# Loads of r and k without their pad rows, one more load in flight, and a re-drawn instruction order, in an RWKV-like attention fused with a gated MLP

## The chip, the cores and the metric

The kernel runs on one core of a Trainium2 chip. The metric is the time of one execution in microseconds (us) on the device; before the change three executions took 326.5, 326.91 and 327.86 us, median 326.91 us. All data are float32.

## What is computed

For 4 batches of 768 tokens, 8 heads of 48 dimensions run a linear recurrence over the tokens; its output, with the heads side by side, goes through a feed-forward layer that mixes along the tokens:

```python
for t in range(S):
    cur = np.einsum('bhd,bhe->bhde', u[None] * kt, vt)
    y[:, :, t] = np.einsum('bhd,bhde->bhe', rt, state + cur)
    state = w[None, :, :, None] * state + np.einsum('bhd,bhe->bhde', kt, vt)
...
h = np.maximum(x @ w_in, 0.0)                     # 384 -> 1024
u, v = h[..., :512], h[..., 512:]
v_n = (v - mean(v)) / sqrt(var(v) + 1e-06)
v_s = np.einsum('ts,bsd->btd', w_spatial, v_n) + b_spatial[None, :, None]
return (u * v_s) @ w_out                          # 512 -> 384
```

## The kernel before

**The work.** The recurrence is done in 24 chunks `m` of 128 tokens, six to a batch. Chunk `m` needs four loads: `rk` (r and k, dimension-major: 128 partitions of 4 KB, 512 KB), `rs` and `ks` (r and k, token-major, 192 KB each) and `rkv` (v, 384 or 512 KB). In `rk` each half of 64 partitions holds one head of each pair: 48 rows of data and 16 rows of zeros, which `dmajor` in `kernel` pads. `prep` (L587) then scales `rk` by powers of w, the k part on POOL (L595) and the r part on DVE (L597) in the first 13 chunks, in one DVE instruction (L601) later; forms `rs*ks*ub` (POOL L353 twice), reduces it per head on DVE (L607), scales `ks` (POOL L353) and spreads the sums on the tile `a` (L353). PE computes `scores` (L638, 32 small matmuls of rk with rk), `products` (L657, of ks with rkv) and `apply` (L719, 64 to 96 matmuls into the tile xp), and `fin` writes the result as a high and a low part, the tile x.

**The layer.** Every large product is done as three matmuls of high and low parts (`mm3`, L762 to L764): `moe_v` (L772, nine of 128x512), `moe_u` (L880, nine of 128x384; the first of all by parts at L892), the token mixing `moe_sp` (with combinations of quadrants, whose weights `wa`, `wb` are split in two parts by ACT and POOL, and whose inputs `t` are split by ACT and POOL or DVE at L358 and L353) and `moe_out`. The weights arrive as 64-bit words; `from_f64` (L475) turns w_in's six pieces of 512 KB into two parts on DVE, ACT and, for three of them, PE (L495 to L497).

**What sets the order.** Nothing runs in the order of the text. Every instruction is a task in `Plan` with the engines it may run on and a cost; `Plan.run` lists the tasks by due times, with models of the transfers (`landing`, with `SLOW`, `PART`, `TO_BYTE`), of PE's clock and its instruction loading, and writes each engine's program in that order. `shake` first moves the due times of random groups of tasks: one group for each number in `SEEDS`, so the numbers in that table set the order. All loads are issued by SP in the planned order (`load`, L367). `LANES` is the number of loads in flight: `run` adds a wait to every load for the one `LANES` loads before it (L300), and `lane` (L213) gives the planner the same rule. A load also waits until its buffer is free; `rk` has two buffers (`SLOTS`), rotated by `tile_of`.

**Names.** In the rows, `rk`, `rs`, `ks`, `rkv`, `wa`, `wb`, `t`, `X`, `a`, `A`, `x`, `xp`, `ps`, `pm` are tiles; `wa<-w_in` and `wb<-w_sp` are loads of weights. PE's L762 with x and wi is `moe_v` or `moe_u`, with wa or wb and t it is `moe_sp`.

Of the kernel before, what the change touches and what calls it, by code (L numbers as in the profile page):

```python
# [8 lines left out]
F32 = mybir.dt.float32  # L9
# [3 lines left out]
ALU = mybir.AluOpType  # L13
AX = mybir.AxisListType

B, H, S, D = 4, 8, 768, 48
# [3 lines left out]
P = 128  # L20
C = 128
# [3 lines left out]
NP = H // 2  # L25
# [14 lines left out]
LEAN = 4.0  # L40
AHEAD = 0.3
ALONE = 1000.0
CALM, LATE = 80.0, dict(DVE=1.0, SP=1.0)
SEEDS = (786675, 590737, 650567, 473966, 410529, 555426, 907183, 123843, 647820, 960324, 828658, 912501, 134089,
         159232, 4393, 523669, 612611, 964576, 241432, 346394, 906374, 371707, 92393, 507276, 798277, 338735, 176835,
         444512, 896537, 239246, 993420, 861971, 866320, 990367, 131959, 191835, 802215, 648123, 562279, 390339,
         978361, 670519, 812235, 451845, 697243, 382570,)
BIAS = dict(DVE=3.0, ACT=3.5)
MOST_IN, MOST_OUT = 2, 1

# [3 lines left out]
CHAIN = dict(PE=0.0, DVE=0.115, ACT=0.11, POOL=0.0, SP=0.0)  # L54
SWITCH = {"bs": 0.095, "br": 0.095, "by": 0.095, "sb": 0.215, "sy": 0.11, "rb": 0.105, "yb": 0.105}
STAY = 1.0
LANES = 6
PORT = dict(DVE=(0.07, 0.0, 0.0), POOL=(0.15, 0.06, 0.02))


# [58 lines left out]
class Plan:  # L119
# [1 line left out]

    SLOW, PART = 210e3, (6.0, 42.0)
    RATE, TO_BYTE, BEHIND_BYTE = (395e3, 395e3, 262e3), (2.2, 2.9, 1.3), (0.5, 0.5, 0.4)

    def __init__(self, slots, wait):
        self.wait, self.sent = wait, []
# [45 lines left out]
    def shake(self):  # L174
        for seed in SEEDS:
            rnd = random.Random(seed)
# [27 lines left out]
    def landing(self, line, at, nbytes):  # L204
        part = sum(at > x for x in self.PART)
        line = max(line, at + self.TO_BYTE[part])
        slow = min(nbytes / self.SLOW, max(0.0, 5.2 - line))
        line += slow + (nbytes - slow * self.SLOW) / self.RATE[part]
        return line, line + self.BEHIND_BYTE[part]

# [2 lines left out]
    def lane(self, at, landed):  # L213
        return max(at, landed[-LANES]) if len(landed) >= LANES else at

    def run(self):
# [8 lines left out]
        while ready:  # L225
# [71 lines left out]
            if way.nbytes:  # L297
                self.sent.append(made.ins)
                if len(self.sent) > LANES:
                    self.wait(made.ins, self.sent[-1 - LANES].name)  # L300
        assert all(t.end is not None for t in self.tasks)
# [3 lines left out]
def fused_kernel(ctx, tc, rkT, rkvE, rkvL, wT, uB, w_in, w_sp, b_sp, w_out, out):  # L305
# [9 lines left out]
    SLOTS = dict(rk=2, rs=2, ks=2, rkv=3, a=1, A=2, t=4, X=2, gt=4, u=8, vs=2, g=3, ob=2, pm=5, ps=1, xp=1, x=2, s=2, t1=1, dg=2, q=2)  # L315
    SLOTS |= {f"w{x}{n}": 1 for x in "ab" for n in range(NS)}
    const = ctx.enter_context(tc.tile_pool(name="const", bufs=1))
# [7 lines left out]
    plan = Plan(SLOTS, wait)  # L325
    T = {}

    def tile_of(key, shape, dtype=F32):
        key = key[:2]
        if key not in T:  # L330
            home = psum if key[0] in ("pm", "ps", "xp") else sbuf
            T[key] = home.tile(shape, dtype, name=key[0], tag=f"{key[0]}{plan.slot[key]}")
        return T[key]
# [6 lines left out]
    def dve(n, f, r, w, cost=None, two=False, due=None):  # L340
        plan.add([("DVE", n / 960 + 0.07 if cost is None else cost, f, two)], r, w).most = due
# [25 lines left out]
    def load(key, shape, dtype, src, nbytes, view=None, due=None):  # L367
        def f():
            t = tile_of(key, shape, dtype)
            return nc.sync.dma_start(out=view(t) if view else t, in_=src)  # L370
        plan.add([("SP", 0.45, f, False, nbytes)], (), [key], lag=0).most = due


    wt = const.tile([P, NP], F32, name="wt")
    ub = const.tile([P, DM], F32, name="ub")
    tt = const.tile([P, NP, C], F32, name="tt")
# [14 lines left out]
    def eye():  # L391
        return tile_of(EYE, [P, P])

    def neg(n=1):
        return tile_of(NEG, [P, 2, P], F32R)[:, n]
# [65 lines left out]
    TTP = ("pm", "tt")  # L461
    TN = [("c", "tn", 0), ("c", "tn", 1)]

    def load_chunk(m):
        b, c = divmod(m, NC)
        load(("rk", m), [P, 2, NP, C], F32, rkT[b, c], P * 2 * NP * C * 4)
        n, src = (ROW_E, rkvE[m]) if m < EC else (ROW, rkvL[m - EC])
        load(("rs", m), [P, DM], F32, src[:, 0:DM], P * DM * 4)
        load(("ks", m), [P, DM], F32, src[:, OK:OV], P * DM * 4)
        load(("rkv", m), [P, ROW - OV], F32, src[:, OV:n], P * (n - OV) * 4, lambda t: t[:, 0:n - OV])  # L470
# [116 lines left out]
    def prep(m):  # L587
        RK, RS, KS, DG, A = ("rk", m), ("rs", m), ("ks", m), ("dg", m), ("a", m)
        a = lambda: tile_of(A, [P, 2, 2, 2, HC])
        r_, k_, kn, rn = (RK + ("r",), RK + ("k",), KS + ("kn",), RS + ("rn",))  # L590
        rk = lambda: T[RK]
        TT = [("c", "t0"), ("c", "t1"), ("c", "t2")]
        if m < EARLY:
            for i, key in ((1, k_), (0, r_)):
                plan.add([("POOL", 1.24, lambda i=i: nc.gpsimd.tensor_tensor(  # L595
                    out=rk()[:, i], in0=rk()[:, i], in1=tt, op=ALU.mult), True),
                    ("DVE", 0.6, lambda i=i: nc.vector.tensor_tensor(  # L597
                        out=rk()[:, i], in0=rk()[:, i], in1=T[TTP].rearrange("p (n c) -> p n c", n=NP),
                        op=ALU.mult), False, 0, LEAN if i else -9.0)], [RK, TTP, *TT], [key])
        else:  # L600
            dve(1024, lambda: nc.vector.tensor_tensor(out=rk(), in0=rk(), in1=tt.unsqueeze(1).to_broadcast(  # L601
                [P, 2, NP, C]), op=ALU.mult), [RK, *TT], [r_, k_], cost=1.14, two=True)
        n_, k0 = (lambda: T[RS]), (lambda: T[KS])
        lean = ALONE if m < QUIET else LEAN
        pair(DM, lambda: dict(out=n_(), in0=n_(), in1=k0(), op=ALU.mult), [RS, KS], [rn], lean=lean)
        pair(DM, lambda: dict(out=n_(), in0=n_(), in1=ub, op=ALU.mult), [rn, ("c", "ub")], [rn], lean=lean)
        dve(DM - 8, lambda: nc.vector.tensor_reduce(out=tile_of(DG, [P, H]), in_=n_().rearrange("s (h d) -> s h d", h=H),  # L607
                                                axis=AX.X, op=ALU.add), [rn], [DG])
        pair(DM, lambda: dict(out=k0(), in0=k0(), in1=tn_f, op=ALU.mult), [KS, rn, *TN], [kn], lean=lean)
        pair(432, lambda: dict(  # L610
            out=a().rearrange("s b q z t -> s (b q z) t"), in0=diag.unsqueeze(1).to_broadcast([P, H, HC]),
            in1=T[DG].unsqueeze(2).to_broadcast([P, H, HC]), op=ALU.mult), [DG, ("c", "diag")], [A], lean=lean)
        if m >= EC:
            move(RK + ("r",), ("A", m), "r", [(64 * (1 - t), t, slice(2 * b, 2 * b + 2), 64 * (t ^ b))
                                              for b in range(2) for t in range(2)],
                 lambda p, h: rk()[h:h + 64, 0, p])
# [422 lines left out]
    for i in range(NM):  # L1039
        n = FIRST[i] if i < NC else len(steps) if i == NM - 1 else int(10 + (i - 5) * per / 6)  # L1040
# [20 lines left out]
    for b in range(B):  # L1061
        for c in range(NC):
            m = b * NC + c
# [93 lines left out]
```

## Time and profile before

| | before |
|---|---|
| three executions | 326.5, 326.91, 327.86 us |
| the profiled execution | 327.6 us, span 325.9 us |
| mean granted clock of PE | 0.995 |
| PE busy | 309.7 us, 95% |
| DMA, mean over the span | 151 GB/s, 49.14 MB |
| 24 loads of rk | 512 KB each, median 5.6 us from issue to landing |

The span runs from the first to the last instruction. PE is busy nearly all the time, so what counts is where it isn't, and what releases it there. A row of the waits or of a timeline tells how long an engine stood idle and which instruction ended that; "issue" is idle time that the profile gives no instruction for. The granted clock is a share of 2.4 GHz.

### The profile page before, as it was taken

The page shows a single profiled execution, that of the slowest core. Times are in us where ns is not written, and L with a number is a line of the kernel's source. Part 1 is how long each engine was busy: PE and PEld are TensorE (multiplying, and loading weights), DVE is VectorE, ACT ScalarE, POOL GpSimd, SP SyncE. Part 2 cuts the span into 40 slices and gives each one's busy share as a digit, 9 for nine tenths or more (in the row PEclk, how much of TensorE's full clock was granted, in tenths as well). Part 3 has the DMA queues.
Part 4 walks back from the last instruction along what each step waited for, and adds up shares of the span by engine and source line. Part 5 has one row for each costly group of instructions (what it writes and reads, how often), then busy time and mean ns, then how long its engine had stood idle before and what let it go on. Part 6 is the DMA issues. An engine that isn't in the chain of part 4 may idle for free.

```text
span 325.9 us, 10933 instructions
## 1 busy us (share of the span) xinstructions
PE 309.7 (95%) x4574; PEld 283.3 (87%) x4574; DVE 245.4 (75%) x465; ACT 198.6 (61%) x492; POOL 250.9 (77%) x235
## 2 busy tenths in 40 slices
PE   2787999999999999999999999999999999999995
PEld 1466788999999888998979998999988989999995
DVE  6899986799962899858999996489998431727830
ACT  4346984847643887767759477686576663433422
POOL 3878999999988999899999875688999440358700
PEclk9997999999999999999999999999999999999999
DMA  6999768685255836154346245264140010010013
GB/s 229 377 393 382 257 219 278 217 295 181 91 172 185 270 100 235 32 178 141 106 166 203 51 177 171 81 205 139 51 147 5 25 50 2 0 51 24 0 42 105
DMA packets 21233, 49.14 MB, mean 151 GB/s; under 512 B 2496, under 2 KB 12096, under 8 KB 21184
## 3 DMA queue, kind: packets, MB, share of 16 engines
q1 hardware_dynamic: 21040, 48.34, 43.2%
q8 instruction: 36, 0.59, 0.8%
q14 instruction: 13, 0.11, 0.1%
q10 hardware_dynamic: 144, 0.10, 0.1%
HBM read 43.58 MB, written 4.72 MB: 148 GB/s over the span
## 4 chain that ended last, share of the span: by engine, by line
PE 68%; DVE 10%; POOL 8%; DMA 7%; ACT 3%; issue 2%; SPq 0%; POOLq 0%; ACTq 0%; DVEq 0%
PE pm L762 20%; PE pm L764 19%; PE pm L763 19%; PE xp L719 5%; DMA rs<-rkvE 4%; PE ps L638 3%; POOL rs L353 2%; DMA rk<-rkT 2%; DMA wb<-w_sp 2%; PE ps L657 1%; DVE rk L601 1%; POOL wb L353 1%; DVE A L625 1%; POOL t L353 1%; DVE a L353 1%
## 5 line engine op out<-in xcount | busy, mean ns | idle before, releaser
L762 PE MATMUL pm<-wa,t 128*128 128x384 f32 x120 | 41.3, 344 | 0.0
L763 PE MATMUL pm<-wa,t 128*128 128x384 f32 x120 | 40.5, 337 | 0.0
L764 PE MATMUL pm<-wa,t 128*128 128x384 f32 x120 | 40.4, 336 | 0.0
L353 POOL TENSOR_TENSOR t<-vs,t 128x384 fp32r<-128x384 f32 x26 | 32.6, 1269 | 1.4 <-ACT t L358 1.4
L762 PE MATMUL pm<-x,wi_h 128*128 128x384 f32 x93 | 32.0, 344 | 0.0
L764 PE MATMUL pm<-x,wi_l 128*128 128x384 f32 x93 | 31.2, 336 | 0.0
L763 PE MATMUL pm<-x,wi_h 128*128 128x384 f32 x93 | 31.2, 336 | 0.0
L624 ACT COPY A<-rk 64x256 f32<-64x256 f32 x54 | 21.8, 404 | 15.1 <-PE xp L719 5.3
L353 POOL TENSOR_TENSOR rs<-rs,ks 128x384 f32<-128x384 f32 x21 | 26.8, 1276 | 4.4 <-DMA ks<-rkvL 2.9
L762 PE MATMUL pm<-wi_h,x 128*128 128x512 f32 x69 | 28.5, 413 | 0.3 <-DVE g L933 0.3
L762 PE MATMUL pm<-wo_h,gt 128*128 128x384 f32 x84 | 28.6, 340 | 0.0
L764 PE MATMUL pm<-wo_h,gt 128*128 128x384 f32 x84 | 28.3, 336 | 0.0
L763 PE MATMUL pm<-wo_l,gt 128*128 128x384 f32 x84 | 28.3, 336 | 0.0
L764 PE MATMUL pm<-wi_h,x 128*128 128x512 f32 x69 | 27.7, 401 | 0.0
L763 PE MATMUL pm<-wi_l,x 128*128 128x512 f32 x69 | 27.5, 399 | 0.0
L353 POOL TENSOR_TENSOR ks<-ks,tn 128x384 f32<-128x384 f32 x23 | 25.1, 1092 | 0.0
L353 POOL TENSOR_TENSOR rs<-rs,ub 128x384 f32<-128x384 f32 x22 | 23.4, 1062 | 1.3
L353 POOL TENSOR_TENSOR X<-vs,X 128x384 f32<-128x384 f32 x9 | 10.6, 1175 | 17.6 <-ACT vs L844 17.2
L933 DVE TENSOR_TENSOR g<-pm,bb 128x384 f32<-128x384 f32 x32 | 17.5, 549 | 8.6 <-PE pm L764 8.2
L353 POOL TENSOR_TENSOR a<-diag,dg 128x512 f32<-128x512 f32 x16 | 17.2, 1077 | 8.5 <-ACT A L624 7.6
L353 POOL TENSOR_TENSOR gt<-u,gt 128x384 fp32r<-128x384 f32 x20 | 22.6, 1142 | 1.3 <-ACT gt L358 1.3
L762 PEld LDWEIGHTS pm<-wa,t 128*128 128x128 f32 x120 | 22.6, 188 | 1.1 <-DVE g L933 0.6
(182 smaller groups left out, 960.4 us busy)
## 6 DMA issues: line engine op xcount, KB each, us to landing
rk<-rkT SPq DMA_DIRECT2D x24, 512.0 KB, 5.6
rkv<-rkvL SPq DMA_DIRECT2D x16, 512.0 KB, 3.8
out<-ob SPq DMA_DIRECT2D x23, 192.0 KB, 2.0
wa<-w_in SPq DMA_DIRECT2D x6, 512.0 KB, 5.5
rkv<-rkvE SPq DMA_DIRECT2D x8, 384.0 KB, 5.9
rs<-rkvL SPq DMA_DIRECT2D x16, 192.0 KB, 2.7
ks<-rkvL SPq DMA_DIRECT2D x16, 192.0 KB, 5.2
wb<-w_sp SPq DMA_DIRECT2D x6, 384.0 KB, 5.4
```

Of the source, the lines that this page charges most:

```text
L353: plan.add([(e, cost[e], lambda e=e: engine[e].tensor_tensor(**f()), True, 0, lean if e == "DVE" else 0.0) for e in ways.split()], r, w)
L601: dve(1024, lambda: nc.vector.tensor_tensor(out=rk(), in0=rk(), in1=tt.unsqueeze(1).to_broadcast([P, 2, NP, C]), op=ALU.mult), [RK, *TT], ...
L624: ("ACT", (n + 250) / 1200, lambda out=out, p=p, h=h: nc.scalar.copy(out(), source(p, h))),
L625: ("DVE", n / 1920 + 0.15, lambda out=out, p=p, h=h: nc.vector.tensor_copy(out=out(), in_=source(p, h)), True, 0, LEAN)],
L638: nc.tensor.matmul(ps[64 * hf:64 * hf + 64, b, o:o + HC], rk[hd, 1, p, s0:s0 + 64], rk[hd, 0, p, t0:t0 + 64], start=True, stop=True, skip_ ...
L657: nc.tensor.matmul(ps[64 * j:64 * j + D, b, o:o + D], kn[hs, kc:kc + D], ve[hs, h, z, p, slice(0, D) if m < EC else slice(16 * h, 16 * h + ...
L719: nc.tensor.matmul(xp[32 * p:32 * p + 32, o:o + HC], lhsT, rhs, start=p not in began, stop=True, skip_group_check=True, tile_position=(0, ...
L762: nc.tensor.matmul(o, lh, rh, start=first, stop=False, skip_group_check=free)
L763: nc.tensor.matmul(o, lh, rl, start=False, stop=False, skip_group_check=free)
L764: nc.tensor.matmul(o, ll, rh, start=False, stop=last, skip_group_check=free)
L933: dve(TH, lambda: nc.vector.tensor_tensor(out=g(K), in0=T[PM][:, 0:TH], in1=other(), op=ALU.add), [PM, ("c", "bb"), *r], [K])
```

## The change

The first load into each of the two `rk` buffers (chunks 0 and 1) brings all 128 rows. From chunk 2 on, `load_chunk` makes two loads, of rows 0 to 47 and 64 to 111, 192 KB each; the pad rows in the buffer stay as they are. For this the two buffers become fixed tiles (`pairs`) and the instructions that read `rk` depend on both loads. `LANES` goes from 6 to 7. In the planner's model of the transfers two constants and the bound 5.2 change, all for the first 6 us, and `SEEDS` is another list of 61 numbers instead of 46, so that every engine's order is another.

```diff
-LANES = 6
+LANES = 7
...
-    SLOW, PART = 210e3, (6.0, 42.0)
-    RATE, TO_BYTE, BEHIND_BYTE = (395e3, 395e3, 262e3), (2.2, 2.9, 1.3), (0.5, 0.5, 0.4)
+    SLOW, PART = 240e3, (6.0, 42.0)
+    RATE, TO_BYTE, BEHIND_BYTE = (395e3, 395e3, 262e3), (0.95, 2.9, 1.3), (0.5, 0.5, 0.4)
...
-        slow = min(nbytes / self.SLOW, max(0.0, 5.2 - line))
+        slow = min(nbytes / self.SLOW, max(0.0, 6.0 - line))
...
     def tile_of(key, shape, dtype=F32):
         key = key[:2]
+        if key[0] == "rk":
+            return T.setdefault(key, pairs[plan.slot[key]])
...
+    pairs = [const.tile([P, 2, NP, C], F32, name=f"rk{n}") for n in range(SLOTS["rk"])]
...
     def load_chunk(m):
         b, c = divmod(m, NC)
-        load(("rk", m), [P, 2, NP, C], F32, rkT[b, c], P * 2 * NP * C * 4)
+        if m < SLOTS["rk"]:
+            load(("rk", m), [P, 2, NP, C], F32, rkT[b, c], P * 2 * NP * C * 4)
+        else:
+            for h in range(2):
+                rows = lambda t, h=h: t[64 * h:64 * h + D]
+                load(("rk", m, h), [P, 2, NP, C], F32, rows(rkT[b, c]), D * 2 * NP * C * 4, rows)
...
-                        op=ALU.mult), False, 0, LEAN if i else -9.0)], [RK, TTP, *TT], [key])
+                        op=ALU.mult), False, 0, LEAN if i else -9.0)], [RK, RK + (0,), RK + (1,), TTP, *TT], [key])
...
-                [P, 2, NP, C]), op=ALU.mult), [RK, *TT], [r_, k_], cost=1.14, two=True)
+                [P, 2, NP, C]), op=ALU.mult), [RK, RK + (0,), RK + (1,), *TT], [r_, k_], cost=1.14, two=True)
```

`SEEDS` starts with 786675, 590737, 650567 before and with 510017, 789016, 349449 after.

What this does to the order, at three places. First SP's loads around those of chunks 2 and 3. Before, from the end of chunk 2's loads to chunk 3's `rk` (`rk_445`; the number behind a name tells the buffers' uses apart):

```order
L370 DMA rk_292<-rkT 128x1024
L370 DMA rkv_301<-rkvE 128x768
L370 DMA rs_311<-rkvE 128x384
L370 DMA wb2_348<-w_sp 128x768
L370 DMA ks_354<-rkvE 128x384
L370 DMA wb1_369<-w_sp 128x768
L370 DMA wb5_429<-w_sp 128x768
L370 DMA rs_434<-rkvE 128x384
L370 DMA wb0_437<-w_sp 128x768
L370 DMA rk_445<-rkT 128x1024
```

The same stretch of SP in the change, from chunk 2's `ks` on:

```order
L373 DMA ks_242<-rkvE 128x384
L373 DMA wb4_291<-w_sp 128x768
L373 DMA rk0_74<-rkT 48x1024 x2
L373 DMA rs_330<-rkvE 128x384
L373 DMA rkv_348<-rkvE 128x768
L373 DMA ks_359<-rkvE 128x384
L373 DMA wb0_365<-w_sp 128x768
L373 DMA wb2_424<-w_sp 128x768
L373 DMA wb5_428<-w_sp 128x768
L373 DMA wb3_434<-w_sp 128x768
L373 DMA wb1_438<-w_sp 128x768
L373 DMA rk1_75<-rkT 48x1024 x2
```

All six pieces of w_spatial now stand ahead of chunk 3's `rk`, four did before. Up to and with chunk 3's `rk` SP asked for 10114 KB before and asks for 10434 KB now; with chunk 2's `rk` it was 7106 and is 7362 KB, with chunk 2's `ks` 6082 and 6594 KB, with chunk 0's `rk` 1538 KB (the fourth load) and 2306 KB (the eighth).

Second PE at chunk 3. Before, from chunk 2's `apply` (the second row of L719 is its a part) to chunk 3's; the nine rows of `moe_v` of chunk 2 (`pm_635`) are cut to their first and last:

```order
L719 MATMUL xp_527<-a_442,rkv_193 32x64 x24
L657 MATMUL ps_81<-rkv_301,ks_354 48x48 x16
L638 MATMUL ps_81<-rk_445 64x64 x16
L762 MATMUL pm_635<-wi_h_82,x_294 128x512
L764 MATMUL pm_635<-wi_h_82,x_294 128x512
L719 MATMUL xp_657<-rk_445,A_114 32x64 x24
L719 MATMUL xp_657<-a_612,rkv_301 32x64 x24
L892 MATMUL pm_718<-x_294,wi_h_82 128x384 x6
```

The same place in the change, where the nine rows are those of `pm_612`:

```order
L728 MATMUL xp_519<-a_466,rkv_175 32x64 x24
L666 MATMUL ps_83<-rkv_348,ks_359 48x48 x16
L771 MATMUL pm_612<-wi_h_84,x_295 128x512
L773 MATMUL pm_612<-wi_h_84,x_295 128x512
L647 MATMUL ps_83<-rk1_75 64x64 x16
L901 MATMUL pm_654<-x_295,wi_h_84 128x384 x4
L728 MATMUL xp_664<-rk1_75,A_120 32x64 x24
L728 MATMUL xp_664<-a_601,rkv_348 32x64 x24
```

Chunk 3's `scores`, which need its `rk`, now stand behind chunk 2's `moe_v` instead of ahead of it, and four of the first `moe_u`'s matmuls stand ahead of chunk 3's `apply`. At chunk 2, `products` now stand ahead of `scores`, the other way round before.

Third POOL at the start of batch 1's token mixing, where the inputs t are made from v (`vs`). Before:

```order
L353 TENSOR_TENSOR vs_1707<-vs_2081,vs_1707 128x3x128
L353 TENSOR_TENSOR t_2432<-X_2416,t_2432 128x384
L353 TENSOR_TENSOR t_2436<-vs_2081,t_2436 128x384
L353 TENSOR_TENSOR wb5_2224<-X_2414,wb4_2186 128x384
L353 TENSOR_TENSOR X_2536<-vs_2081,X_2416 128x384
L353 TENSOR_TENSOR X_2554<-vs_1707 128x384
L353 TENSOR_TENSOR t_2556<-X_2536,t_2556 128x384
```

In the change:

```order
L356 TENSOR_TENSOR wb5_2370<-X_2402,wb4_2344 128x384
L356 TENSOR_TENSOR X_2467<-vs_1767 128x384
L356 TENSOR_TENSOR X_2491<-vs_2084,X_2467 128x384
L356 TENSOR_TENSOR t_2511<-X_2467,t_2511 128x384
L356 TENSOR_TENSOR t_2514<-vs_2084,t_2514 128x384
L356 TENSOR_TENSOR vs_1767<-vs_2084,vs_1767 128x3x128
L356 TENSOR_TENSOR X_2491<-vs_2084,X_2491 128x384
```

The last split of a weight (`wb5`) stands ahead of all of these instead of among them, the input of the fourth product (`X_2536` before, `X_2491` now) is made three instructions earlier, and its split is no longer on POOL.

## Rows read from the trace of the kernel before

**Rows 1.** page part 1: engine, busy us (share of the span), instructions
```profile
PE 309.7 (95%) x4574; PEld 283.3 (87%) x4574; DVE 245.4 (75%) x465; ACT 198.6 (61%) x492; POOL 250.9 (77%) x235
```

**Rows 2.** stretches of the span, their columns named in the first row
```profile
core 0: us, PE busy (x) PEld busy (x) DVE busy (x) ACT busy (x) POOL busy (x), PEclk, DMA share, GB/s
0.00:35.03 35.03, 23.64 (x583) 16.88 (x583) 30.49 (x59) 18.42 (x45) 25.67 (x37) 0.95 0.94 347
35.03:326.00 290.97, 286.08 (x3993) 266.41 (x3992) 214.94 (x407) 180.16 (x448) 225.18 (x199) 1.00 0.38 127
```

**Rows 3.** waits of PE after 35 us: engine line <- releaser: us, times, longest
```profile
PE pm L764 <- POOL t L353: 0.8, 1, 0.8
PE pm L762 <- DVE g L933: 0.3, 1, 0.3
```

**Rows 4.** stretches of 4 us and the last 6 us (columns as in group 2)
```profile
24.00:28.00 4.00, 1.94 (x67) 1.72 (x68) 4.00 (x9) 2.00 (x7) 3.66 (x5) 0.86 1.02 381
28.00:32.00 4.00, 4.00 (x61) 3.00 (x60) 3.96 (x9) 3.38 (x10) 3.59 (x4) 0.71 1.02 383
320.00:326.00 6.00, 2.27 (x13) 1.95 (x12) 0.36 (x1) 0.80 (x2) 0.00 (x0) 1.00 0.26 89
```

**Rows 5.** timeline of PE: start us, us, instruction xcount [idle before <-releaser]
```profile
25.34 0.30 PE L719 MATMUL xp<-a,rkv 128*32 128x64 f32 x2 [1.59 <-issue]
...
26.36 0.73 PE L638 MATMUL ps<-rk 64*64 64x64 f32 x32 [0.72 <-issue]
...
27.66 0.79 PE L762 MATMUL pm<-wi_h,x 128*128 128x512 f32 x1
...
33.01 0.58 PE L657 MATMUL ps<-rkv,ks 64*48 64x48 f32 x32
...
34.34 0.69 PE L638 MATMUL ps<-rk 64*64 64x64 f32 x32 [0.76 <-POOL rk L595]
...
34.97 0.50 PE L762 MATMUL pm<-wi_h,x 128*128 128x512 f32 x1
...
38.73 1.32 PE L892 MATMUL pm<-x,wi_h 128*128 128x384 f32 x6
```

**Rows 6.** chain that ended last, first 40 us: start us, us, piece
```profile
2.18 6.12 DMA rk<-rkT
```

**Rows 7.** tile rk on SP, 17.5 to 17.9 us: issue, then its time to landing
```profile
L370 SPq DMA_DIRECT2D rk<-rkT x1: 328/328/328, 17.6 to 17.6; - x1
...
DMA to landing us min/median/max: 6.0/6.0/6.0
```

**Rows 8.** tile rk on SP, 25.99 to 26.31 us, the same
```profile
L370 SPq DMA_DIRECT2D rk<-rkT x1: 328/328/328, 26.0 to 26.0; - x1
...
DMA to landing us min/median/max: 6.9/6.9/6.9
```

**Rows 9.** timeline of POOL, the start
```profile
21.16 1.02 POOL L353 TENSOR_TENSOR rs<-rs,ks 128x384 f32<-128x384 f32 x1 [1.27 <-DMA ks<-rkvE]
...
24.19 1.27 POOL L595 TENSOR_TENSOR rk<-rk,tt 128x512 f32<-128x512 f32 x1
...
25.72 1.04 POOL L353 TENSOR_TENSOR a<-diag,dg 128x512 f32<-128x512 f32 x1 [0.26 <-PE xp L719]
...
31.18 1.01 POOL L353 TENSOR_TENSOR wa<-wb,wa 128x384 fp32r<-128x384 f32 x1 [0.41 <-ACT wa L358]
...
33.01 1.27 POOL L595 TENSOR_TENSOR rk<-rk,tt 128x512 f32<-128x512 f32 x1 [0.82 <-DMA rk<-rkT]
```

**Rows 10.** timeline of POOL, 144 to 149 us
```profile
144.38 1.01 POOL L353 TENSOR_TENSOR wb<-X,wb 128x384 fp32r<-128x384 f32 x1
...
147.62 1.35 POOL L353 TENSOR_TENSOR t<-X,t 128x384 fp32r<-128x384 f32 x1
```

**Rows 11.** tile A on SP: its two 64-row DMAs of 64 KB, time to landing
```profile
L623 SPq DMA_DIRECT2D A<-rk x2: 462/498/534, 66.6 to 67.4; - x2
...
DMA to landing us min/median/max: 3.7/3.9/4.2
```

More of the change, by code (lines that the diff above doesn't have):

```diff
@@ L43 @@
 CALM, LATE = 80.0, dict(DVE=1.0, SP=1.0)
[L44 to L47, printed above, removed]
+SEEDS = (510017, 789016, 349449, 4415, 22282, 162314, 413315, 599960, 460165, 632294, 15888, 576524, 887186, 388971,
[4 rows of a table added]
 BIAS = dict(DVE=3.0, ACT=3.5)
```

4 rows, old and new, of the table SEEDS are left out of this document.

## The prediction

> **What bounds the kernel now.** I read the page's busy times first: PE works 309.7 us of a span of 325.9 us [rows 1], so 16.2 us are all that an order of instructions can still win. The stretches tell where they lie [rows 2]: in the first 35.03 us PE is idle for 11.4 us, in the other 290.97 us for 4.9 us. The waits of PE in that long part [rows 3] name only 0.8 us behind a POOL instruction and 0.3 us behind a DVE instruction; 3.7 us of the rest are the copy and the store after the last matmul, in the last 6 us [rows 4], which the change leaves as they are. So the long part is bound by PE's own work, which the change does not touch: the same matmuls, in another order. A time can come out differently by the first 35 us, by those 1.1 us, or by new waits.
>
> In the first 35 us the DMA engines are the bound: their share is 1.02 from 24 to 32 us [rows 4] and 0.94 over all of the stretch [rows 2], and what PE and POOL wait for are loads. POOL stood 1.27 us until chunk 2's `ks` had landed, and 0.82 us until chunk 3's `rk` had [rows 9]; PE waited 0.76 us for that `rk` to be scaled by POOL [rows 5]. Ahead of that it had stood 1.59 and 0.72 us with no instruction named ("issue") [rows 5], and then the granted clock fell: 0.86 and 0.71 of full speed from 24 to 32 us [rows 4], 1.00 in all that comes later [rows 2]. That is 4 x 0.14 + 4 x 0.29 = 1.7 us of PE's work lost at the lower level, 1.2 GHz.
>
> **The change part by part.** *When the loads land.* I take the landings as a function of the kilobytes that SP has asked for. Chunk 0's `rk` completes 1538 KB and lands at 2.18 + 6.12 = 8.3 us [rows 6]; chunk 2's 7106 KB at 17.6 + 6.0 = 23.6 us [rows 7]; chunk 3's 10114 KB at 26.0 + 6.9 = 32.9 us [rows 8]. That is 5568 KB in 15.3 us, 364 KB/us, and then 3008 KB in 9.3 us, 323 KB/us. With the new list: chunk 2's `ks` (6594 KB) lands at 8.3 + 5056/364 = 22.2 us, its `rk` (7362 KB) at 23.6 + 256/323 = 24.4 us, chunk 3's `rk` (10434 KB) at 23.6 + 3328/323 = 33.9 us; at 364 KB/us it would be 32.7 us. So at the place that matters the smaller loads bring nothing earlier: 2 x 128 KB are saved up to there, but two more pieces of w_spatial, 768 KB, have been put ahead.
>
> *Chunk 0's `rk`* lands 768 KB later, 2.1 us. I cost it at nothing: 4288 KB, 11.8 us of transfers, lie between it and the next load that anything waited for, chunk 2's `ks`. Without that cover it costs up to 2.1 us.
>
> *Chunk 2.* POOL starts on it at 22.2 instead of 21.16 us; three instructions later, 24.19 - 21.16 = 3.03 us, it scales `rk`, at 25.2, which takes 1.27 us [rows 9]. `scores` can start at 26.5 us; they started at 26.36 us [rows 5], 0.9 us after POOL was done. I call that level; the hold before them stays, since it stands at the same place of PE's program, and with it the lower clock.
>
> *Chunk 3, the term of the sum.* `products` of chunk 2 now run ahead of `scores`, while POOL still scales `rk`, so `moe_v` of chunk 1 starts at about 26.5 + 0.6 = 27.1 instead of 27.66 us. From there to the end of chunk 3's `products` it took 33.01 + 0.58 - 27.66 = 5.9 us [rows 5], so they end at 33.0 us. Before, PE now had `scores` of chunk 3 in front of it and waited. In the change it has chunk 2's `moe_v`. That and chunk 3's `apply` took 38.73 - 34.97 = 3.8 us, the `scores` 0.6 us, four of the six matmuls at L892 about 0.8 us [rows 5]; x of chunk 2 comes about 0.3 us late. The sum is 33.0 + 5.5 = 38.5 us, with the four matmuls done. Before, `apply` ended at 38.73 us and the four came behind it: 39.5 us. The gain is 1.0 us, and 1.3 us if x is in time; I take **1.2 us**. `scores` don't wait: POOL has as many instructions ahead of chunk 3's scaling as before (8.0 us from 24.19 to 32.19 us [rows 9], so free by 33.2 us), starts it when `rk` lands, 33.9 us, and ends it at 35.2 us, when `moe_v` ends too. Its bounds: nothing, if `rk` lands 1.2 us later than that; 2.9 us, if the clock stays up as well.
>
> *Seven in flight* I cost at nothing: with six the engines' share was already 1.0 [rows 4]. *22 more loads* on SP take 0.33 us each [rows 7]; SP waits between loads there, so they are hidden, and not if a load behind them is due, 0.33 us at a time. *Later chunks:* 20 x 128 KB fewer, at a DMA share of 0.38 [rows 2], are worth nothing.
>
> *The two late waits.* The 0.8 us were for the split of t that POOL began at 147.62 us; the split of a weight that stood in its way ran from 144.38 us for 1.0 us [rows 10]. In the change that one is ahead of the group, the input is made three instructions earlier, and the split has left POOL. I take **0.8 us** as gained, and leave the 0.3 us behind DVE; the bounds are 1.1 us gained and 1.1 us lost, as much again in new waits.
>
> *Sum.* The profiled execution of 327.6 us would become 327.6 - 1.2 - 0.8 = 325.6 us. It was 0.7 us above the median of the three runs, 326.9 us, so the forecast for the median is **324.9 us**, 0.6% less. About 0.5%, 1.6 us, is what a measurement of this kernel can tell from no change.
>
> **The rivals.** *The gain turns into other waits.* The new order has every instruction elsewhere, and POOL is busy for 225 of the later 291 us, DVE for 215 [rows 2], so neither can catch up quickly; `rk` of chunk 3 may land late, or the late waits come back at another product. For it speaks that each of the two terms is only about 1 us; against it that the long part had only 1.1 us of waits with the old order. Time: 326.9 less one of the terms or none, 325.7 to 326.9 us. Chance 0.28.
>
> *A load of 48 rows moves at half the rate*, and so the kernel gets slower. Then the pair of chunk 2 and that of chunk 3 take 384/182 = 2.1 us each instead of 1.05 us at 364 KB/us, and chunk 3's `rk` lands 2.1 us later, at 36.0 us. POOL has it scaled at 37.3 us, PE stands from 35.4 us for 1.9 us, `apply` ends at 40.2 instead of 39.5 us, and PE's stand is about as long as the 1.59 + 0.72 us after which the clock fell before [rows 5], worth another 1.7 us. With none of the gains that is 326.9 + 0.7 + 1.7 = 329.3 us. It decides from a landing of chunk 3's `rk` at 35 us on. For it: the only transfers of half the rows in the trace, 64 KB each, took 3.7 and 4.2 us to land [rows 11], with an eighth of the bytes of a load that took 6.0 us [rows 7]. Against it: these are two copies inside the chip, and the two halves of a pair are in flight together and go to different rows. Chance 0.12. The Trainium skill, "SBUF — State Buffer", section "Door 1: The DMA port swizzle", has such a rule: rows 0 to 63 are reached through only 8 of the 16 ports, and a transfer to them gets little more than half the bandwidth; rows 64 to 127 use the other 8. [...]
>
> *The clock does not fall.* If PE's stand ahead of chunk 2's `scores` gets shorter, since `products` now come first and fill part of it, the granted clock may stay at 2.4 GHz. Against it: `ks` of chunk 2 lands a microsecond later than before. Time: 324.9 - 1.7 = 323.2 us. Chance 0.10.
>
> That the change doesn't save bytes can be left out: the order shows 48 rows per half in all chunks from the third on.
>
> **How the numbers follow.** The forecast, both terms within about a microsecond, has 0.50. Below 325.3 us (faster by over 0.5%) lie seven tenths of it, the rival with the clock and hardly anything of the first rival: 0.46. Above 328.5 us lie most of the slow loads and a little of the rest: 0.11. Between them 0.43. The range takes in the clock's rival below and stops short of the slow loads' full price above: 322.9 to 328.2 us. The likeliest case alone spans 323.9 to 325.9 us.
>
> **What would show it.** In the profile after: chunk 3's `apply` ends by 38.5 us with four matmuls of `moe_u` ahead of it; `scores` of chunk 3 follow `moe_v` of chunk 2 with no idle time named POOL; chunk 3's second half lands between 32.7 and 34 us; the granted clock falls once more, between 24 and 32 us; PE's waits after 35 us add up to less than 0.5 us. I am wrong in the first term if PE waits for POOL's scaling of `rk` there, in the second if a new wait of PE of 0.5 us or more stands anywhere behind 40 us, and in the whole if a pair of halves takes longer to land than a load of 512 KB did.

## The result: 1.3% slower, and the profile after

The changed kernel takes 331.44 us (median of four runs, 330.87 to 331.54), before takes 326.94 us beside it: a ratio of 1.013, interval 1.0106 to 1.0155. The forecast was 324.9 us, its range ended at 328.2 us, and the case "slower" had been given 0.11. The profiled execution took 331.49 us with a span of 329.7 us.

The stretches of the changed kernel that answer to [rows 4] (columns as there), with two longer ones:

```profile
24.00:28.00 4.00, 1.52 (x64) 1.10 (x56) 3.55 (x8) 1.95 (x6) 3.92 (x5) 0.92 0.96 321
28.00:32.00 4.00, 4.00 (x45) 2.98 (x41) 3.64 (x9) 3.22 (x8) 3.92 (x5) 0.65 0.95 296
20.00:40.00 20.00, 15.88 (x435) 12.22 (x429) 16.79 (x34) 13.61 (x37) 14.34 (x14) 0.91 0.99 295
80.00:100.00 20.00, 19.39 (x222) 17.96 (x222) 18.14 (x39) 10.63 (x30) 15.80 (x16) 1.00 0.72 184
```

The two longer ones of before:

```profile
20.00:40.00 20.00, 16.84 (x488) 13.65 (x478) 19.01 (x37) 14.91 (x40) 17.00 (x17) 0.91 0.92 342
80.00:100.00 20.00, 20.00 (x229) 19.20 (x228) 15.88 (x33) 8.78 (x23) 17.49 (x18) 1.00 0.36 119
```

From 24 to 32 us the DMA engines are nearly as full as before (0.96 and 0.95 against 1.02), but move 321 and 296 GB/s where they moved 381 and 383 [rows 4]; from 20 to 40 us they are fuller and move 295 instead of 342. The granted clock lost 4 x 0.08 + 4 x 0.35 = 1.7 us, as before, so between these two profiles the clock is not the difference.

The same seen from the queue of loads, in the page's part on DMA queues (packets, MB, share of 16 engines over the span), first of before, then of the change:

```profile
q1 hardware_dynamic: 21040, 48.34, 43.2%
```

```profile
q1 hardware_dynamic: 20928, 45.72, 46.6%
```

Fewer bytes, more engine time: 0.432 x 325.9 = 140.8 us for 48.34 MB against 0.466 x 329.7 = 153.6 us for 45.72 MB. The 44 new loads carry 8.65 MB; if the other 37.07 MB still cost 140.8/48.34 = 2.91 us per MB, they took 108.0 us and the halves 45.6 us, 5.3 us per MB, **1.8 times the price of a byte before**. A quarter of the bytes of r and k was saved, and their engine time rose from 11.53 x 2.91 = 33.6 to 45.6 us.

This is where it reaches PE first. Tile `rk` on SP, the issue of chunk 3's two halves and their time to landing (as [rows 8]):

```profile
L373 SPq DMA_DIRECT2D rk<-rkT x2: 327/350/372, 26.7 to 27.1; - x2
...
  DVE rk L606: 1.6, 1
  POOL rk L604: 1.2, 1
...
DMA to landing us min/median/max: 8.2/8.4/8.5
```

A pair takes 8.2 to 8.5 us to land, where the one load of 512 KB took 6.9 us [rows 8]; the second half is in at about 27.1 + 8.4 = 35.5 us. POOL and DVE both stand for it. The timelines of POOL, DVE and PE there:

```profile
23.20 1.02 POOL L356 TENSOR_TENSOR rs<-rs,ks 128x384 f32<-128x384 f32 x1 [3.60 <-DMA ks<-rkvE]
...
35.76 1.28 POOL L604 TENSOR_TENSOR rk<-rk,tt 128x512 f32<-128x512 f32 x1 [1.18 <-DMA rk<-rkT]
37.00 1.00 POOL L356 TENSOR_TENSOR rs<-rs,ks 128x384 f32<-128x384 f32 x1
```

```profile
36.13 0.69 DVE L606 TENSOR_TENSOR rk<-rk,pm 128x512 f32<-128x512 f32 x1 [1.57 <-DMA rk<-rkT]
...
37.59 0.36 DVE L713 TENSOR_TENSOR ps<-ps,t 128x192 f32<-128x192 f32 x1
```

```profile
27.54 1.13 PE L647 MATMUL ps<-rk 64*64 64x64 f32 x32 [0.66 <-POOL rk L604]
...
33.35 0.57 PE L666 MATMUL ps<-rkv,ks 64*48 64x48 f32 x32
...
38.06 0.69 PE L647 MATMUL ps<-rk 64*64 64x64 f32 x32 [1.55 <-POOL rs L356]
38.68 0.96 PE L901 MATMUL pm<-x,wi_h 128*128 128x384 f32 x4
...
40.27 0.85 PE L728 MATMUL xp<-a,rkv 128*32 128x64 f32 x48
```

`scores` of chunk 3 start at 38.06 us, and the row names POOL's product `rs`. That name is a coincidence: the product ended at 38.00 us, DVE's sum on `ps` (L713) at 37.95. In the kernel with 64 rows below (experiment 3) the product and the sum lie further apart, and the row names the sum:

```profile
39.69 0.69 PE L647 MATMUL ps<-rk 64*64 64x64 f32 x32 [2.36 <-DVE ps L713]
```

The same POOL product ends there at 39.72 us, behind this start, and in the kernel with 112 rows (experiment 9) at 37.83, where `scores` start at 37.62 us. So what `scores` wait for is L713, which writes the tile that `scores` write: it stands behind the scaling of `rk` (L606) on DVE, and that one stood for the load. Chunk 3's `apply` ends at 41.1 us, with four matmuls of `moe_u` done, against 39.5 us before.

Behind 35 us PE's waits are these (as [rows 3]):

```profile
PE ps L647 <- POOL rs L356: 1.6, 1, 1.6
PE pm L771 <- DVE g L942: 0.9, 2, 0.7
PE pm L771 <- DVE wo_l L515: 0.5, 1, 0.5
PE pm L773 <- DVE x L765: 0.4, 1, 0.4
PE pm L772 <- DVE wo_l L515: 0.3, 1, 0.3
PE pm L771 <- DVE x L361: 0.2, 1, 0.2
```

They add up to 3.9 us, where it was 1.1. The old 0.8 us for t are gone; new ones stand at other places. The chain that ended last shows what lies ahead of those for `wo_l` (start us, us, piece):

```profile
78.53 8.88 DMA rk<-rkT
87.49 0.69 DVE rk L606
...
96.64 0.47 DVE wo_l L515
...
103.08 0.48 DVE wo_l L515
103.60 0.44 PE pm L772
```

A pair of halves took 8.88 us to land in a stretch where the engines were at 0.72, at 184 GB/s (before: 0.36 and 119). DVE stood 1.1 us for it, and what stands behind it in DVE's order came late: some 9 us later PE stands for a part of a weight that has nothing to do with r and k. This holds for the wait of 0.5 us; the one of 0.3 us on L772 stands in both profiles of experiment 8 too, where no half is loaded, so it isn't the halves' doing alone.

### The profile page after: what moved, and what is told of

The parts are those of the page before. It is cut to its first block, busy times and chain, and to the rows that moved or that the text cites. A ratio compares the mean times of both kernels' runs of the same rounds, so it can differ in the third digit from the quotient of the medians.

```text
span 329.7 us, 10993 instructions
## 1 busy us (share of the span) xinstructions
PE 311.8 (95%) x4574; PEld 282.8 (86%) x4574; DVE 235.9 (72%) x461; ACT 199.0 (60%) x491; POOL 251.8 (76%) x237
## 3 DMA queue, kind: packets, MB, share of 16 engines
q1 hardware_dynamic: 20928, 45.72, 46.6%
## 4 chain that ended last, share of the span: by engine, by line
PE 53%; POOL 18%; DMA 17%; DVE 8%; issue 2%; SPq 1%; ACT 0%; POOLq 0%; DVEq 0%
PE pm L771 16%; PE pm L773 15%; PE pm L772 15%; DMA rk<-rkT 8%; POOL t L356 4%; PE xp L728 4%; DMA ks<-rkvE 3%; POOL rs L356 3%; POOL X L356 3%; DMA wa<-w_in 3%; POOL wb L356 2%; PE ps L647 2%; DMA rs<-rkvE 2%; DMA ks<-rkvL 1%; SPq L373 1%
## 5 line engine op out<-in xcount | busy, mean ns | idle before, releaser
L772 PE MATMUL pm<-wa,t 128*128 128x384 f32 x120 | 40.4, 337 | 0.0
L356 POOL TENSOR_TENSOR rs<-rs,ks 128x384 f32<-128x384 f32 x20 | 24.9, 1247 | 14.3 <-DMA ks<-rkvL 5.2
L356 POOL TENSOR_TENSOR t<-vs,t 128x384 fp32r<-128x384 f32 x26 | 31.7, 1236 | 3.1 <-ACT t L361 3.1
L772 PE MATMUL pm<-x,wi_h 128*128 128x384 f32 x93 | 31.2, 335 | 0.0
L356 POOL TENSOR_TENSOR a<-diag,dg 128x512 f32<-128x512 f32 x20 | 22.7, 1137 | 9.5 <-ACT A L633 5.8
L356 POOL TENSOR_TENSOR gt<-u,gt 128x384 fp32r<-128x384 f32 x21 | 24.3, 1168 | 5.8 <-ACT gt L361 5.7
L772 PE MATMUL pm<-wo_l,gt 128*128 128x384 f32 x84 | 28.3, 337 | 0.3 <-DVE wo_l L515 0.3
L772 PE MATMUL pm<-wi_l,x 128*128 128x512 f32 x69 | 27.5, 398 | 0.0
L633 ACT COPY A<-rk 64x256 f32<-64x256 f32 x48 | 19.4, 405 | 9.5 <-PE xp L728 6.3
L771 PEld LDWEIGHTS pm<-wa,t 128*128 128x128 f32 x120 | 22.6, 188 | 1.7 <-DVE g L942 0.7
L610 DVE TENSOR_TENSOR rk<-rk,tt 128x1024 f32<-128x1024 f32 x11 | 17.7, 1613 | 8.7 <-DMA rk<-rkT 8.6
L356 POOL TENSOR_TENSOR rs<-rs,ub 128x384 f32<-128x384 f32 x20 | 22.5, 1125 | 1.0
L356 POOL TENSOR_TENSOR u<-g,u 128x384 f32<-128x384 f32 x18 | 20.5, 1141 | 3.3 <-DVE g L942 2.6
L772 PEld LDWEIGHTS pm<-wa,t 128*128 128x128 f32 x120 | 22.5, 188 | 0.1
```

Source lines behind the costliest of these rows:

```text
L356: plan.add([(e, cost[e], lambda e=e: engine[e].tensor_tensor(**f()), True, 0, lean if e == "DVE" else 0.0) for e in ways.split()], r, w)
L633: ("ACT", (n + 250) / 1200, lambda out=out, p=p, h=h: nc.scalar.copy(out(), source(p, h))),
L771: nc.tensor.matmul(o, lh, rh, start=first, stop=False, skip_group_check=free)
L772: nc.tensor.matmul(o, lh, rl, start=False, stop=False, skip_group_check=free)
```

## The experiments

The times of before beside these runs are medians of 327.8 to 328.5 us, so the ratios carry the comparison. Two theories from the start: (A) a transfer whose rows all lie in one half of the 128 costs the engines far more per byte; (C) the new order is to blame. (B), small transfers, and (D), the seventh load in flight, stand beside them.

**1. Loads alone.** This kernel computes nothing of the reference; it only loads, up to seven in flight, in eight stages. Rows 0 to 47 and 64 to 111 in turn are `t[64 * (i % 2):64 * (i % 2) + 48]`, the other stages are like it. It was executed once.

> This kernel computes nothing of the reference: it only makes loads, seven in flight, in eight stages that wait for each other, and stores a tile of zeros and copies at the end. Theory A (a load whose rows lie in one half of the partitions, 0 to 47 or 64 to 111, moves at about half the rate because only half of the ways into the memory serve it): loads of all 128 rows with 4 KB each move at 370 to 400 GB/s, loads of rows 0 to 47 alone at 180 to 220, loads of rows 40 to 87, which lie on both sides, at 260 to 330, and loads of all rows with 1.5 or 2 KB each at 350 or more; rows 0 to 47 and 64 to 111 in turn lie between 200 (each load slow for itself) and 380 (the two sides make up for each other). Theory B (small loads are slow, whatever their rows): all loads of 192 KB, also those of all rows with 1.5 KB, move at 200 to 280 GB/s. Theory C (loads of 48 rows are as fast as any, the slow landings of the changed kernel come from its order): all stages within 15% of the first.

Stretches inside the eight stages, in their order (us, DVE, POOL, clock, DMA share, GB/s): 128 rows of 4 KB; halves of 48 rows in turn; rows 0 to 47; rows 40 to 87; halves of 64 rows in turn; 128 rows of 2 KB; 112 rows of 2 KB; 128 rows of 1.5 KB.

```profile
8.00:20.00 12.00, 1.66 (x3) 0.00 (x0) 1.00 1.02 407
30.00:46.00 16.00, 0.00 (x0) 0.00 (x0) 1.00 1.04 223
56.00:78.00 22.00, 0.00 (x0) 0.00 (x0) 1.00 1.05 155
88.00:100.00 12.00, 0.00 (x0) 0.00 (x0) 1.00 1.04 292
108.00:130.00 22.00, 0.00 (x0) 0.00 (x0) 1.00 1.04 227
140.00:150.00 10.00, 0.00 (x0) 0.00 (x0) 1.00 1.04 371
158.00:174.00 16.00, 0.00 (x0) 0.00 (x0) 1.00 1.05 266
182.00:192.00 10.00, 0.00 (x0) 0.00 (x0) 1.00 0.99 319
```

The share is 1 in all of them: the engines are always full, and the rate differs by 2.6 times. Rows 0 to 47 and rows 40 to 87 are as many, as long and as many bytes, and go at 155 and 292 GB/s: what counts is where the rows lie. A pair of 48-row halves costs 2 x 197 KB / 223 GB/s = 1.76 us, the 512 KB load that it replaces 524 KB / 407 = 1.29 us. Size is a part of it (192 KB on all rows: 319), the rows the larger one (192 KB in halves: 223). One half over and over gives 155, so a pair in turn makes up some of it and not all. And 112 rows give less than 128: 229 KB take 0.86 us, 262 KB on all rows 0.71. Two stages lie outside what was expected under (A), 155 (180 to 220) and 319 (350 or more); (B) asked for 200 to 280 in all stages of 192 KB, (C) for no difference over 15%.

**2. All rows, in two transfers.** In the changed kernel each of the two loads brings all 128 rows of r or of k.

```diff
-                rows = lambda t, h=h: t[64 * h:64 * h + D]
+                rows = lambda t, h=h: t[:, h]
```

> The changed kernel in its own order, every instruction at its place, but each of the two loads of a chunk brings all 128 rows of r or of k, 2 KB a row, 256 KB, instead of 48 rows of both, 192 KB: a third more bytes, the same number of loads. Theory A (half the rows, half the rate): rk of chunk 3 lands at about 34.5 instead of 36.1 us, scores of chunk 3 start near 36.5 instead of 38.06 us, the wait of PE for the DVE instruction wo_l at 96 and 103 us goes, and the time falls from 331.4 to 327.5 to 329 us. Theory B (small loads) and theory C (the order): 331 to 333 us, since nothing but more bytes is added.

327.53 us (ten runs, 324.72 to 328.37), ratio 0.9986, interval 0.9955 to 1.0018. With a third more bytes of r and k the loss is gone: for (A), against (B) and (C). In its profile (325.24 us, span 323.5) the pair of chunk 3 lands in 6.2 us, DVE has no wait at that place, and `scores` follow `moe_v` at once. Tile `rk` on SP, DVE and PE there:

```profile
DMA to landing us min/median/max: 6.2/6.2/6.3
```

```profile
33.24 0.68 DVE L606 TENSOR_TENSOR rk<-rk,pm 128x512 f32<-128x512 f32 x1
...
34.70 0.36 DVE L713 TENSOR_TENSOR ps<-ps,t 128x192 f32<-128x192 f32 x1
```

```profile
34.88 0.40 PE L773 MATMUL pm<-wi_h,x 128*128 128x512 f32 x1
35.21 0.69 PE L647 MATMUL ps<-rk 64*64 64x64 f32 x32
35.83 0.97 PE L901 MATMUL pm<-x,wi_h 128*128 128x384 f32 x4
...
37.42 0.85 PE L728 MATMUL xp<-a,rkv 128*32 128x64 f32 x48
```

That is the picture that the forecast had drawn for the change: `apply` ends at 38.3 us (38.5 was forecast). Later, DVE's waits for `rk` on line 606 behind 40 us are, in this kernel and then in the changed one (us, times, longest):

```profile
DVE rk L606 <- DMA rk<-rkT: 1.9, 3, 1.1
```

```profile
DVE rk L606 <- DMA rk<-rkT: 6.4, 4, 2.3
```

Its ten runs lie in two groups, four at 324.7 to 325.8 and six at 327.5 to 328.4 us; the profile is of the first group, and what sets the second apart isn't seen. Before spreads as widely: 29 executions of it beside experiment 11 took 325.8 to 330.2 us, so a difference of 2 us between two single profiles shows nothing by itself.

**3. Halves of 64 rows.**

```diff
-                rows = lambda t, h=h: t[64 * h:64 * h + D]
+                rows = lambda t, h=h: t[64 * h:64 * h + 64]
```

> The changed kernel in its own order, with rows 0 to 63 and 64 to 127 in the two loads of a chunk, 256 KB each: the same bytes and the same number of loads as the kernel with all rows of r or k per load, but each load in one half of the partitions. Theory A: slower than the changed kernel by a third more time in each pair, about 0.7 us at each of chunks 2 and 3 and as much where a load is late in the middle: 332 to 334 us. Theory B: like the kernel with all rows per load, within 0.8 us. Theory C: 331 to 332 us.

338.14 us, ratio 1.0336, interval 1.0274 to 1.0399: the same bytes as in experiment 2, the same number of loads, only cut by rows instead of columns, and 3.5% apart. This is the plainest proof of (A). Queue 1's share is 49.8%, with all rows 45.3%. The price was larger than the 332 to 334 us expected, and part of it is the clock: behind the stand of 2.36 us shown above the granted clock is 0.62 from 40 to 44 us, where the changed kernel, after 1.55 us, has 1.00.

**4. Six in flight** in the changed kernel (the seventh before becomes the sixth, in the emission alone, so the order stays).

```diff
-                if len(self.sent) > LANES:
-                    self.wait(made.ins, self.sent[-1 - LANES].name)
+                if len(self.sent) > 6:
+                    self.wait(made.ins, self.sent[-7].name)
```

> The changed kernel in its own order, but each load waits for the one six loads before it, as in the kernel before. Theory A: in the first 40 us fewer loads share the engines, the bytes per us stay, so the landings stay within 0.5 us and the time within 0.8 us of 331.4 us. A rival, theory D (the seventh load in flight takes bandwidth from the loads that are due, so they land late): the loads of chunks 2 and 3 land 1 us or more earlier and the time falls below 330 us.

332.91 us (two runs), ratio 1.0176 (1.012 to 1.0232): not faster. (D), which asked for less than 330 us, falls.

**5. The halves in the old order.** Before's kernel with two things changed: r and k come in halves from chunk 2 on, and seven loads are in flight instead of six.

```diff
+                for one in made if isinstance(made, list) else [made]:
+                    self.sent.append(one.ins)
+                    if len(self.sent) > 7:
+                        self.wait(one.ins, self.sent[-8].name)
...
+            if key[0] == "rk" and key[1] >= SLOTS["rk"]:
+                return [nc.sync.dma_start(out=t[64 * h:64 * h + D], in_=src[64 * h:64 * h + D]) for h in range(2)]
```

> The order of before, with only the load of r and k changed: from chunk 2 on rows 0 to 47 and rows 64 to 111 in two transfers, each load waiting for the seventh before it. If the halves themselves cost the time (A), it is slower than before by 2.5 to 6 us, 330 to 334 us: 44 loads that leave the engines at 223 GB/s where all rows go at 371 to 407, and chunk 3's r and k land near 36 us instead of 33. If it is the new order that is bad (C), it is within 1 us of before, 327 to 328.5 us. A rival to both: the old order asks for its loads earlier or later and so hides them, then 327 too, but the rate in 28:36 us would still be under 310 GB/s.

331.91 us, ratio 1.0138 (1.0103 to 1.0174): as slow as the whole change, in the order of before. (C) falls. Seven in flight by themselves make this order a little faster (experiment 11, 0.9957), so here the halves cost 1.0138/0.9957, 1.8%. From 20 to 40 us its engines move 298 GB/s at a share of 1.01, where before had 342 at 0.92. The loss lies at other places than expected: POOL starts on chunk 3's `rk` at 33.55 us, 0.5 us behind before and not near 36, and the granted clock, which was 0.91 from 20 to 40 us in the profile of before, is 1.00 in this one. Later PE waits at places where before's kernel doesn't, 0.8 us at 59.56 us and 0.7 us at 123.88 us among them; how each comes from a half wasn't traced.

**6 and 7. The halves late, the halves early.** All rows for chunks 2 and 3 and halves from chunk 4 on (`late48`); then the converse (`front48`).

```diff
-                rows = lambda t, h=h: t[64 * h:64 * h + D]
+                rows = (lambda t, h=h: t[:, h]) if m < 4 else (lambda t, h=h: t[64 * h:64 * h + D])
```

> The changed kernel, but chunks 2 and 3 bring all 128 rows of r, then of k (256 KB each); from chunk 4 on the 48-row halves as changed. If the loss is made at two places, 2 us before 41 us by late loads at the front and 2 us between 75 and 105 us by a halves' load that DVE waits for (A), this gives 328.5 to 330 us, with chunk 3's scores right behind moe_v of chunk 2, and with the waits for wo_l at 96 and 103 us still there. If the front is everything and the later waits only follow from it, 327 to 328 us. If the later halves are everything, 331 us.

> The converse of the version with late halves: chunks 2 and 3 in 48-row halves as changed, from chunk 4 on all 128 rows of r, then of k. If the losses at the two places add up, as the traces have it (the changed kernel's scores of chunk 3 start 2.8 us behind those of the version with all rows at the front, and 2.3 us more are lost where chunk 10's scores wait behind late loads), this stays about 2.5 us behind the version with all rows everywhere: 329.5 to 331 us, scores of chunk 3 at about 38 us, no wait for wo_l between 96 and 105 us. If the later order makes the front's delay up, 327 to 328.5 us.

Late: 329.08 us, ratio 1.0031 (0.9995 to 1.0067). Early: 329.40 us, 1.0053 (1.0026 to 1.0079), and in its profile `scores` of chunk 3 start at 37.62 us, 0.1 us behind the end of L713 again. Against all rows everywhere (0.9986) that is 1.5 and 2.2 us, 3.7 of the 4.7 us between 0.9986 and 1.013; the rest is within the intervals. So the loss is made at both places. The early one is clear of the noise; the late one is not by its interval, which overlaps that of all rows, and rests on the trace too. The late kernel's waits for `wo_l` (timeline of PE), which the early one has none of:

```profile
94.79 0.50 PE L771 MATMUL pm<-wi_h,x 128*128 128x512 f32 x1 [1.20 <-DVE wo_l L515]
...
101.25 0.45 PE L772 MATMUL pm<-wo_l,gt 128*128 128x384 f32 x1 [0.29 <-DVE wo_l L515]
```

**8. The new order without halves**, with one transfer of all rows and 512 KB in the place of the first half and none in that of the second; seven in flight stay.

```diff
-                rows = lambda t, h=h: t[64 * h:64 * h + D]
+                rows = (lambda t: t) if not h else None
...
```

> The changed kernel's order with one transfer of all 128 rows of r and k (512 KB, as before had it) in the place of the first half, and none in the place of the second. This is the new order alone. Theory A: 325 to 328 us, as the load of all rows in two transfers (327.5), a little less if anything since the 512 KB go at 407 GB/s against 371. If two smaller transfers instead of one help by themselves, it is 1 us or more above the version with two transfers of all rows.

327.02 us, ratio 0.9971 (0.9942 to 1.0000). Once more, with more runs:

> The new order with one transfer of all rows once more, in more rounds: 326.4 to 327.6 us, a ratio to before of 0.997 to 1.000 with its interval touching 1 or just below. So the order alone is worth a microsecond at most; were it worth the 2.0 us of the forecast, the ratio would be 0.994.

327.92 us, 0.9983 (0.9952 to 1.0014). Order and seven in flight together are worth a microsecond at most, and no different from experiment 2's. The ends of chunk 3's `apply` (timelines of PE, the first run, then the second):

```profile
38.51 0.85 PE L730 MATMUL xp<-a,rkv 128*32 128x64 f32 x48
```

```profile
38.80 0.85 PE L730 MATMUL xp<-a,rkv 128*32 128x64 f32 x48
```

With the four matmuls of `moe_u` done that is 39.4 and 39.6 us, as late as before's 39.5.

**9. Rows 0 to 111.**

```diff
-                rows = lambda t, h=h: t[64 * h:64 * h + D]
+                rows = lambda t, h=h: t[0:112, h]
```

> The changed kernel's order with rows 0 to 111 of r, then rows 0 to 111 of k: 224 KB each, an eighth less than all rows. By bytes (the planner's way of counting) it is at or under the version with all rows, 326 to 327.5 us. By the loads alone, where 224 KB on 112 rows went at 266 GB/s (0.86 us each) and 256 KB on 128 rows at 371 (0.71 us each), it is slower than all rows by 1 to 2.5 us, 328.5 to 330 us: chunk 2 and 3 together 0.6 us later at the front, and chunk after chunk the engines are busier.

328.47 us, ratio 1.003 (0.9996 to 1.0064): by the ratios 1.4 us slower than all rows, the way the loads alone had it and against the count of bytes; but the intervals overlap, so in the kernel this isn't shown.

**10. Two queues.** Loads alone again; the lower halves issued by SP, the upper ones by ACT.

```diff
+            one(lambda t, i=i: t[64 * (i % 2):64 * (i % 2) + 48, 0:W], nc.scalar if i % 2 else nc.sync)
```

> Loads alone again, nothing of the reference computed, up to seven in flight. Five stages: all rows in 512 KB (407 GB/s before); 48-row halves in turn on SP's queue (223 GB/s before); the same halves, the lower ones on SP's queue and the upper ones on ACT's; all rows of half the width, 256 KB, in turn on the two queues; rows 0 to 95 in 384 KB on SP. Theory: on one queue an engine works through one transfer after the other, so that the two halves of a pair do not make each other up; then two queues, whose transfers the engines take in turn, bring the halves to 330 GB/s or more, near the 371 of 256 KB loads. Rival: rows of 48 are slow by how the three rows of an engine meet the others', whatever runs beside them; then two queues give 220 to 260. Rows 0 to 95: by ports a mean of the two halves, about 290 to 310; were it only the size, 390.

Halves on one queue, then on two, and rows 0 to 95 (columns as in experiment 1):

```profile
26.00:44.00 18.00, 0.00 (x0) 0.00 (x0) 1.00 1.05 210
52.00:68.00 16.00, 0.00 (x0) 0.00 (x0) 1.00 1.05 208
...
98.00:110.00 12.00, 0.00 (x0) 0.00 (x0) 1.00 1.02 276
```

My theory, that the two halves fail to make each other up because one queue's transfers are worked off one after the other, falls: 208 against 210 GB/s. The same halves on one queue had 223 in experiment 1, so a few per cent between two such runs mean nothing. Rows 0 to 95 stay under both numbers expected for them, 290 to 310 by place and 390 by size.

**11. Seven in flight in the old order**, and nothing else.

```diff
-                if len(self.sent) > LANES:
-                    self.wait(made.ins, self.sent[-1 - LANES].name)
+                if len(self.sent) > 7:
+                    self.wait(made.ins, self.sent[-8].name)
```

> Before's kernel with each load waiting for the seventh before it instead of the sixth, and nothing else. The forecast costed this at nothing: 326 to 328 us, a ratio of 0.998 to 1.002. If a seventh load in flight slows the others, 328.5 us or more; if it brings loads at the front earlier, 325.5 or less.

326.82 us, ratio 0.9957 (0.9930 to 0.9984): the time as expected, the ratio a little below, and the only version whose whole interval lies below 1. Its stretch that answers to the first row of [rows 2]:

```profile
0.00:35.00 35.00, 24.24 (x585) 16.98 (x586) 30.96 (x61) 18.98 (x45) 26.22 (x38) 0.95 0.95 356
```

356 GB/s instead of 347 up to there, and `scores` of chunk 3 at 33.68 instead of 34.34 us. Behind 35 us PE's named waits in this profile are 0.5 us, and none of them is for t.

## Why the prediction was wrong

**What bounds the kernel** was right in the main: the first 35 us belong to the loads, the rest to PE, and the loss came where the loads became dearer; but the part behind 35 us lost by them too.

**The step that failed is "when the loads land".** I took landings as a function of kilobytes asked for, 364 and then 323 KB/us, and put 48-row loads on that line. All loads from which the two rates came were of 128 rows. A 48-row load costs 1.8 times as much per byte in the kernel, and 407/223 = 1.8 times alone. So chunk 3's `rk` landed at about 35.5 us, not 33.9. Chunk 2's `ks`, a load of all rows, let POOL go at 23.20 us, not 22.2; that is only in part the halves', since the same point lies at 21.9 to 22.3 us in the four profiles of this order with all rows at the front and at 22.4 to 23.2 in those with 48, 64 or 112. The sign I had set ("in the whole if a pair of halves takes longer to land than a load of 512 KB did") came true: 8.4 against 6.9 us.

**The term of chunk 3**, 1.2 us gained, became 1.6 us lost (41.1 against 39.5 us). Beside the landing I missed a wait: I had only POOL's scaling ahead of `scores`, but DVE's L713 stands on the same `ps`, behind DVE's own scaling of `rk`: POOL was done at 37.04, `scores` began at 38.06 us. With all rows in two loads the step comes out as drawn, 38.3 us; with all rows in one load it doesn't (experiment 8).

**"Later chunks are worth nothing"** failed for the same reason in the other direction. Dearer bytes there cost about 1.5 us by the medians (experiment 6). A share of 0.38 is an average; from 80 to 100 us it rose to 0.72, and one late load held DVE's whole queue.

**The late waits**, 0.8 us: the one for t went away, but waits for g grew from 0.3 to 0.9 us, and 0.8 us for `wo_l` and 0.6 us for x came. That the order took the one for t away isn't shown: it is gone in the old order with seven in flight too, and 0.5 us for t are back in the first run of experiment 8. PE's named waits behind 35 us, 1.1 us before, are 0.4 us with all rows in two loads, 1.0 and 1.2 us with all rows in one.

**Seven in flight, "nothing"**: before with seven is 0.4% faster (0.2 to 0.7%), and the change with six 0.4% slower by the medians, within the intervals. The argument was that the engines' share was 1.0 already; it was so from 24 to 32 us, not in the whole front.

**The gain itself**, 2.0 us, isn't there. With punctual loads the new order has ratios of 0.997 to 0.999 in three comparisons, with seven in flight among them, and the old order with seven has 0.9957. The one profile that looks like the forecast (experiment 2, a span of 323.5 us) is of the faster group of its runs; the two of experiment 8 have 325.2 and 326.1 us, before 325.9. By these ratios the order with whole loads would take 326.0 to 326.5 us, which is the rival "the gain turns into other waits" (325.7 to 326.9 us, 0.28) and not the forecast.

**The rival that came true** was the load of 48 rows at half the rate. Its first steps hold: landing 36.0 (about 35.5 measured), POOL done at 37.3 (37.04), PE's stand 1.9 us (1.55). That its time, 329.3 us, is only 2.1 us short is in part luck: 1.7 us of it were for a second fall of the clock, and in the changed kernel's profile the granted clock is 1.00 from 32 to 48 us. Instead, the front cost 1.6 and not 0.7 us, with the wait for L713 in it, and the later chunks cost something, which it had left out. It got 0.12 for two reasons. One: the only half-row transfers in the trace, 64 KB in 3.7 to 4.2 us [rows 11], were set aside as copies inside the chip; no run tests what makes them slow, and in the changed kernel's profile four like them land in 2.7 us (median), so they were a hint and no more. Two: the halves of a pair would make each other up. That is refuted: in turn they give 223 GB/s, on two queues 208.

The Trainium skill, "SBUF — State Buffer", section "Door 1: The DMA port swizzle", says that rows 0 to 63 reach only half of the ports. Rows 0 to 47 alone agree with it in direction, 155 against 407 GB/s, though that is less than half; that two halves in turn are at full rate does not follow from it. The skill's "DMA: Bandwidth & Descriptors", section "The descriptor swizzle", says that in a transfer to 128 partitions each engine writes one port of its own. With it would go that fewer rows do worse than 128: 112 rows 266 against 371 GB/s at 2 KB a row, 96 rows 276 and the halves 223 against 407 at 4 KB; no run shows which engine writes which row, so this is an argument and not shown.

## What to carry to other kernels

Price a load by engine time, not by bytes: a rate taken from loads of 128 rows says nothing about loads of 48, and leaving out pad rows here cost more than carrying them. Compare one change at a time before crediting an order: here the old order with one more load in flight did as well as the new one. Where a change brings a shape that no row of the trace has, an argument about its price is worth little; a kernel of loads alone settles it. And a load that comes late is paid for by whatever stands behind it on the engine that waits: look along that engine's order, not only at the tile's own users.

## What was not expected of the hardware

- Rows cut at 64, 48 rows or 64, in turn: 223 to 227 GB/s, whatever the number of rows. The 48 rows from 40 to 87, which lie in both halves, go at 292; rows 0 to 95 at 276; rows 0 to 111 at 266; all 128 at 371 with 2 KB a row and 407 with 4 KB. In every one of these stretches the engines' share is about 1, so a full share says nothing of the rate.
- PE stands for nothing that the profile names ("issue") inside chunk 1's `apply`, in some kernels inside chunk 2's too, while the DMA engines are full: 1.59 us before, 1.54 after, 2.90 with 64 rows, 0.75 with all rows in two loads, but 1.77 and 1.60 with all rows in one and 2.14 in the old order with seven in flight. So it doesn't simply follow the price of the loads; its cause was not tried.
- A releaser named for a wait can be a neighbour that ended within 0.1 us. Two kernels with other delays (64 and 112 rows) told them apart.
